# Moving small steps in an attention and adapter kernel: products ahead of scores at lag changes, counts at the end, sums ahead of an output, one store ahead of another

## The chip, the cores and the metric

The kernel runs on one core of a Trainium2 chip. The metric is the device time of one execution in microseconds (us), as a median of several runs. The profile comes from one further execution, recorded by the hardware profiler. The engines are called PE (TensorE matmuls; its weight loads are listed as PEld), DVE (VectorE), ACT (ScalarE), POOL (GpSimd) and SP (SyncE, which here only issues DMAs). An engine works through its own instructions in program order and waits on semaphores of the others.

## The reference

Four batches of 12,288 queries of width 128 attend to 768 keys each. The keys, which are the values too, are 4x4 means of a 384 x 32 map, multiplied by one 128 x 128 matrix. The attention's result goes through a mixture of eight low-rank adapters of rank 16, of which two are chosen for each row.

```python
kv_pool = kv.reshape(B, H // 4, 4, W // 4, 4, C).mean(axis=(2, 4))
k = v = kv_pool.reshape(B, -1, C) @ w_sr
s = (q @ k.transpose(0, 2, 1)) / np.sqrt(C)
a = softmax(s)
x = (a @ v).reshape(B * N, C)               # 49152 x 128
logits = x @ w_gate                         # 8 experts
topk = the two largest of each row;  w = softmax of their logits
out = x + sum over the two: w_k * ((x @ A[e_k]) @ B[e_k])
```

## The kernel before

**Tiling.** The 49,152 queries are 96 chunks of 512 rows (24 chunks to a batch); chunk numbers below are these, and `n` is the last one, 95. A chunk's work has a first and a second half.

First half: `scores(c, r)` multiplies 256 keys by the 512 queries (two matmuls of 512 columns, L329) into one of two score buffers (`stile`, PSUM), and ACT takes the exponential into `tt` (L330). There are three such pairs a chunk. `weigh(c, h)` multiplies the exponentials by the extended values (the values, seven logit columns and a column of ones) into one PSUM buffer, 12 matmuls for each half `h` (L341). `normalise(c)` on DVE takes the reciprocal of the sums of weights (L348), multiplies (L352, which frees the PSUM buffer) and finds the largest logits (L359). `gate` on POOL (L368 to L372) and `gate_tanhs` on ACT make the two gates of each row.

Second half, some chunks later: `turned` transposes the attention rows on PE (L408) into the bank of `t_bank`, from which DVE (L419), in the end ACT (L417), copies them. `gated_hidden` multiplies by A (L443) and applies the gates on DVE (L446). `up` multiplies by B (L489). `give` adds the attention rows (DVE, L503) and issues the store on SP for each pair of chunks (L522). How many chunks later is the `lag`: 9 at the beginning, then 8, 7 and 6 from chunks 57, 67 and 81 on. Where the lag shrinks by one, two products fall into the same iteration: two `gated_hidden` in iterations 65, 74 and 87 and two `up` in iterations 69, 78 and 91. The first of the two uses the bank of `t_bank`, the second the usual bank (`mtile`).

**Order.** All is written out by hand, in the order in which each engine is to work. In iteration `c` of the main loop PE gets: a pair of scores, `weigh(c-1, 0)`, a pair of scores, the first of two `gated_hidden` (where there are two), `up` (one or two), `weigh(c-1, 1)`, the transposes of chunk `c-2`, a pair of scores, the last `gated_hidden`.

**Checks.** The kernel skips the subtraction of the maximum in the softmax. To be safe it counts, over all rows and batches, whether the sums and the values lie in a safe range: `count_ok` and `values_ok` fill `flags`, `count_sum(0)` adds `flags` over the partitions by a matmul with ones (L568) and a copy on ACT (L569), `count_sum(1)` limits eight of the numbers to 1 (L571) and adds them (L572). The last 15 chunks are judged by `tail_ok` on POOL (L575, L576) and counted by `all_ok` on PE (L580, L581); `flag` (DVE, L585 and L587) compares the total with the full count. At the very end all engines read that flag and skip a slow, exact version.

**The tail.** When the main loop is over (iteration 94 is its last), the score buffers are given back and their space becomes the banks `bank(0)`, `bank(1)` and `y5`. The tail finishes chunks 88 to 95 step by step: `weigh(n-1)` and `weigh(n)`, `tops4` (DVE, L834 to L840) in the place of `normalise`; `gate_args` (POOL, L775 to L778), `gate_tanh` (ACT, L781), `gate_w` (POOL, L788, L789); `hidden` (PE, L819), `gated` (DVE, L794), `turn` (PE, L803, copied by ACT at L809 or DVE at L811), `up`; and then either `add_rows` (DVE, L503), or `take` (ACT copies, L494) and `add` (POOL, L498). `put` issues a store of one chunk (256 KB) on SP (L508); the last chunk's goes on ACT's queue. In the last chunk the copy of the transposes is split between ACT and DVE (L811), its two up products are L913 and L918, and the outputs are made by ACT (L915) and DVE (L919).

Of the kernel before, what the change touches and what calls it, by code (L numbers as in the profile page):

```python
# [21 lines left out]
def kernel(  # L22
# [10 lines left out]
    nc = tc.nc  # L33
# [167 lines left out]
    def stile(name):  # L201
        return ps_s.tile([P, 2, NTOK], FP32, tag="sg", name=name)
# [129 lines left out]
    def weigh(c, h, banks=None):  # L332
        b = c // CPB
        if banks is not None:
            xps[c] = banks
        elif h == 0:
            xps[c] = ps_x.tile([P, 2, 512], FP32, tag="x", name="xps")
        for j in range(h * NH, (h + 1) * NH):
            for s in range(NS):
                o = xps[c][:, s // 2, (s % 2) * VW:(s % 2 + 1) * VW]  # L340
                mm(o, tt[c][:, j, s * P:(s + 1) * P], vext[b][:, j, 0:VW],  # L341
                   start=(j == 0 and s % 2 == 0), stop=(j == NJ - 1 and s % 2 == 1),
                   skip_group_check=True)
# [37 lines left out]
    def gate_tanhs(p):  # L381
        gw[p] = gw_all[:, p % 4].rearrange("p e s -> p s e")
        if p < OWN // 2:
            nc.scalar.activation(gw_all[:, p % 4], garg[p].rearrange("p s e -> p e s"), AF.Tanh,
                                 bias=0.0, scale=0.5)
        else:
            th = small.tile([P, 2 * NS, E], FP32, tag="th", name="th")
            nc.scalar.activation(th, garg[p], AF.Tanh, bias=0.0, scale=0.5)
            nc.gpsimd.tensor_scalar(th, th, 1.0, None, op0=ALU.add)
            gw[p] = th  # L390
# [49 lines left out]
    def gated_hidden(c, bank=None):  # L440

        h_ps = mtile([P, NS, P], name="h_ps") if bank is None else as_tokens(bank)
        mm(h_ps, a_bf, xT[c], start=True, stop=True)  # L443
        hgT[c] = run.tile([P, NS, P], BF16, tag="ht", name="ht", bufs=4)
        h = c % 2 * NS // 2
        nc.vector.scalar_tensor_tensor(  # L446
            hgT[c].rearrange("p (k a) t -> p k (a t)", k=2),
            gE[c // 2][:, h:h + NS // 2].rearrange("p a t k -> p k (a t)"), 1.0,
            h_ps.rearrange("p (k a) t -> p k (a t)", k=2), op0=ALU.add, op1=ALU.mult)
# [16 lines left out]
    def apply_gate(c):  # L466
        new_hg(c)
        g = gw[c // 2][:, (c % 2) * NS:(c % 2 + 1) * NS]
        nc.vector.tensor_tensor(
            hg[c].rearrange("p s (r e) -> p s r e", e=E),  # L470
            hps[c].rearrange("p s (r e) -> p s r e", e=E),
            g.unsqueeze(2).broadcast_to([P, NS, RK, E]),
            op=ALU.mult)
# [10 lines left out]
    def up(c, bank=None):  # L484
        fresh = c not in dps
        if fresh:
            dps[c] = mtile([P, NS, P], name="d_ps") if bank is None else as_tokens(bank)
        for s in range(NS):
            mm(dps[c][:, s], columns(hgT[c], c, s), b_bf, start=(s == 0 and fresh),  # L489
               stop=(s == NS - 1), skip_group_check=True)  # L490
# [6 lines left out]
    def add(c, osb, eng):  # L497
        eng.tensor_tensor(osb, osb, xn[c][:, :, 0:C], op=ALU.add)  # L498
# [65 lines left out]

    def count_sum(step):
        if step == 0:
            cnt_ps = stile("cnt_ps")[0:1, 0, 0:2 + 2 * B]
            mm(cnt_ps, ones_c, flags, start=True, stop=True)  # L568
            nc.scalar.activation(cnt, cnt_ps, AF.Copy)  # L569
        else:  # L570
            nc.vector.tensor_scalar(cnt[:, 2:], cnt[:, 2:], 1.0, None, op0=ALU.min)  # L571
            nc.vector.tensor_reduce(tot, cnt, axis=AX.X, op=ALU.add)  # L572

    def tail_ok():
        nc.gpsimd.tensor_scalar(ok[:, tail], rv[:, tail], 1.0 / L_HI, None, op0=ALU.is_ge)  # L575
        nc.gpsimd.tensor_scalar(low, rv[:, tail], 1.0 / L_LO, None, op0=ALU.is_le)  # L576
# [28 lines left out]
    def t_bank():  # L605
        return ps_t.tile([P, NTOK], FP32, tag="tp", name="t_ps")
# [24 lines left out]
    def next_scores():  # L631
        if todo:
            scores(*todo.pop(0))
# [55 lines left out]
    for c in range(2, NCH - 1):  # L689
        b, k = divmod(c, CPB)  # L690
        if c in fetched and lag(2 * fetched[c] + 1) > 8:
            load_gates(fetched[c])
        if c % 2 == 0 and c // 2 + 3 < 2 * NQ:
            turn_q(c // 2 + 3)
        if c % 2 and (c + 11) // 2 < 2 * NQ:
            load_q((c + 11) // 2)
        if c == 2:
            load_q(6)
        next_scores()
        weigh(c - 1, 0)  # L700
        if c == NCH - 2:
            down(c - 4, stile("h_ps")[:, 0])
            apply_gate(c - 4)
        next_scores()
        if c in tanhs:
            gate_tanhs(tanhs[c])
        for x in made.get(c, ())[:-1]:
            gated_hidden(x, t_bank())
        for x in ups.get(c, ()):
            up(x, None if x == ups[c][-1] else t_bank())  # L710
            give(x)
        if c in fetched and lag(2 * fetched[c] + 1) <= 8:
            load_gates(fetched[c])
        weigh(c - 1, 1)
        prep_step(c)
        if c == CUT + 5:
            count_sum(0)
        normalise(c - 1)
        if c % 2 == 0:
            gate(c // 2 - 1, nc.gpsimd)  # L720
            if c // 2 + 4 < 2 * NQ:
                cast_q(c // 2 + 4)
        _, evacuate = turned("x", c - 2)
        if c == NCH - 2:
            _, evacuate_h = turned("h", c - 4, stile("t_ps")[:, 0])
        next_scores()
        prep(c)
        k0 = 19
        if k in (k0, k0 + 2, k0 + 4) and b + 1 < B:
            if b == 0:  # L730
                squares(0, (k - k0) // 2)
            squares(b + 1, (k - k0) // 2)


        early = max(len(made.get(c + 1, ())), len(ups.get(c + 1, ()))) > 1
        if early:
            evacuate()
        for x in made.get(c, ())[-1:]:
            gated_hidden(x)
        if c in sent:  # L740
            send_gates(sent[c])
        if c == NCH - 2:
            down(c - 3, stile("h_ps")[:, 0])
            apply_gate(c - 3)
        if not early:
            evacuate(c == NCH - 2)
        if c == NCH - 2:
            evacuate_h(True)

        if c in (32, 40, 56, 80):  # L750
            ranges((32, 40, 56, 80).index(c))
        a = slice(0, CUT * NS)
        if CUT < c <= CUT + 3:
            count_ok(a, c - CUT - 1, flags[:, 0:1])
        elif c == CUT + 4:
            values_ok()
        elif c == CUT + 7:
            count_sum(1)

# [5 lines left out]
    def bank(i):  # L767
        return ps_e.tile([P, NTOK], FP32, tag=f"e{i}", name=f"e{i}")
# [22 lines left out]
    def gated(c, lo, hi, g, hb):  # L791
        if c not in hg:
            new_hg(c)
        nc.vector.tensor_tensor(  # L794
            hg[c][:, lo:hi].rearrange("p s (r e) -> p s r e", e=E),
            hb.rearrange("p s (r e) -> p s r e", e=E),
            g[:, lo:hi].unsqueeze(2).broadcast_to([P, hi - lo, RK, E]), op=ALU.mult)
# [33 lines left out]
    def tops4(c, top, y):  # L831
# [7 lines left out]
        for s in range(NS):  # L839
            nc.vector.max(top[:, s], xn[c][:, s, C:C + E])  # L840

    gate_tanhs(q_ - 1)
    y4 = ps_x.tile([P, 2, 512], FP32, tag="x", name="y4")
    weigh(n - 1, 0, y4)
# [9 lines left out]
    def fbank(i):  # L854
        return ps_f.tile([P, NTOK], FP32, tag=f"f{i}", name=f"f{i}")
# [5 lines left out]
    up(n - 6, bank(1))  # L861
    o6 = take(n - 6)
    h2 = hidden(n - 3, 0, NS, mtile([P, NTOK], name="h2"))
    up(n - 5, bank(0))
    gate_args(n - 1, 0, NS, nc.gpsimd, top4, arg4, msk4)
    y5 = ps_e.tile([P, 2, 512], FP32, tag="y5", name="y5")
    weigh(n, 0, y5)
    gated(n - 3, 0, NS, gw[q_ - 1][:, 0:NS], h2)
    put(n - 5, add_rows(n - 5))
    add(n - 6, o6, nc.gpsimd)  # L870
# [7 lines left out]
    o1 = take(n - 4)  # L878
    gate_w(0, NS, nc.gpsimd, arg4, msk4)
    tops4(n, top5, y5)  # L880
    tail_ok()
    turn(hg[n - 3], 0, NS, mtile([P, NTOK], name="t2"), hgT, n - 3)
    h4 = hidden(n - 1, 0, NS, bank(1))
    turn(hg[n - 2], 0, NS, t_bank(), hgT, n - 2)
# [10 lines left out]
    h5 = hidden(n, 0, NS, x3[:, 0])  # L895
    turn(hg[n - 1], 0, NS, bank(1), hgT, n - 1)
    gate_w(0, NS, nc.gpsimd, arg5, msk5)
    gated(n, 0, NS, arg5, h5)
    x_first(n - 1, fbank(1), 2, 4)
    d5 = bank(0)  # L900
    x_first(n, d5, 0, 2)
# [2 lines left out]
    turn(hg[n], 2, 4, t_bank(), hgT, n, False)  # L904
    o4 = take(n - 1)
    put(n - 1, o4)
    add(n - 4, o1, nc.gpsimd)
    put(n - 4, o1)
    count = mtile([P, NTOK], name="count")
    all_ok(count)  # L910
    d5 = dps[n]
    for s in range(2):
        mm(d5[:, s], hgT[n][:, s], b_bf, start=False, stop=(s == 1), skip_group_check=True)  # L913
# [2 lines left out]
    d6 = as_tokens(bank(1))  # L916
    for s in range(2, 4):
        mm(d6[:, s - 2], hgT[n][:, s], b_bf, start=(s == 2), stop=(s == 3), skip_group_check=True)  # L918
    nc.vector.tensor_tensor(o5[:, 2:4], d6[:, 0:2], xn[n][:, 2:4, 0:C], op=ALU.add)  # L919
    put(n, o5, queue=nc.scalar)  # L920
    flag(count)
# [127 lines left out]
```

## Time and profile before

| | |
|---|---|
| median of 3 runs | 371.56 us |
| lowest, highest of the runs | 370.53, 2091.47 us |
| the profiled execution | 371.88 us |
| its span, first to last instruction | 370.1 us |
| mean granted TensorE clock | 0.997 |
| PE busy | 355.1 us, 96% |
| ACT busy | 308.7 us, 83% |
| DVE busy | 299.9 us, 81% |
| POOL busy | 223.8 us, 60% |
| DMA moved | 101.01 MB, mean 273 GB/s |

The middle one of the three runs is the time that counts; the highest is an execution by itself and says nothing of the others. A timeline row has the start in us, the duration in us, the engine, the line of the kernel, the operation, what it writes and reads, its shape and how many instructions are merged in it; in brackets stands how long the engine had been idle before it and which engine and line ended that wait. A row of waits has the total, how many and the longest. Matmuls overlap, so the step from one row's start to the next is the time that PE needs for a row; the duration includes the way through the array. The chain of waits follows the work that ended last, back from the end, piece by piece.

### The profile page before, as it was taken

To read this page: it belongs to the slowest core of one execution; us is meant where nothing else is said; L and a number is where in the kernel's file an instruction comes from. 1 tells how busy PE (TensorE), PEld (TensorE's weight loads), DVE (VectorE), ACT (ScalarE), POOL (GpSimd) and SP (SyncE) were. 2 spreads that over 40 slices of the span, in tenths; PEclk is the share of its full clock that TensorE was granted. 3 is DMA by queue.
4 is the path that set the end of the run, shared out by engine and by line. 5 is a ranking of instruction groups with operands and counts; after the bars stand their busy time and mean duration, and the time that the engine had idled before them with its cause. 6 is when DMAs were issued, how large, how long until landed. Compare 5 with 4: busy or idle time off the path is not lost.

```text
span 370.1 us, 10598 instructions
## 1 busy us (share of the span) xinstructions
PE 355.1 (96%) x3944; PEld 263.6 (71%) x3945; DVE 299.9 (81%) x953; ACT 308.7 (83%) x390; POOL 223.8 (60%) x374
## 2 busy tenths in 40 slices
PE   4889999999999999999999999999999999999984
PEld 1446677777777777777777777777777777777773
DVE  3785558888788888888888888888888889989994
ACT  1569998898988898998988988988888889989843
POOL 1013699989589879685477969784544324323253
PEclk9999999999999999999999999999999999999998
DMA  7998999999999999999999999999768789744324
GB/s 251 421 371 200 297 320 320 297 300 290 282 362 303 311 305 332 313 287 262 282 303 336 318 344 309 294 312 250 236 208 250 253 247 223 229 131 131 147 115 174
DMA packets 83818, 101.01 MB, mean 273 GB/s; under 512 B 58804, under 2 KB 59060, under 8 KB 83764
## 3 DMA queue, kind: packets, MB, share of 16 engines
q1 hardware_dynamic: 83332, 99.98, 92.9%
q8 instruction: 31, 0.51, 0.6%
q10 hardware_dynamic: 432, 0.33, 0.3%
q14 instruction: 23, 0.19, 0.2%
HBM read 62.33 MB, written 25.90 MB: 238 GB/s over the span
## 4 chain that ended last, share of the span: by engine, by line
PE 89%; DVE 3%; ACT 3%; DMA 2%; issue 1%; POOL 1%; SPq 0%; ACTq 0%; DVEq 0%
PE xps L341 36%; PE sg L329 33%; PE t_ps L408 6%; PE d_ps L489 5%; PE h_ps L443 5%; DMA kvt<-in_kv_dram 2%; ACT tt L330 2%; PE v_ps L218 1%; DVE kvt L194 1%; PE k_ps L243 1%; PE w_ps L612 1%; PE kp_ps L210 0%; ACT qT L600 0%; DVE xn_all L352 0%; PE y L341 0%
## 5 line engine op out<-in xcount | busy, mean ns | idle before, releaser
L330 ACT ACTIVATE tt<-sg 128x1024 f16<-128x1024 f32 x288 | 276.7, 1022 | 34.6 <-PE sg L329 33.8
L329 PE MATMUL sg<-qT,kfT 128*128 128x512 f16 x576 | 170.3, 379 | 0.6 <-ACT qT L600 0.3
L341 PEld LDWEIGHTS <-tt 128*128 128x128 f16 x2304 | 146.2, 98 | 28.2 <-DVE xn_all L352 17.8
L341 PE MATMUL xps<-vext,tt 128*128 128x136 f16 x2256 | 164.7, 223 | 0.3 <-DVE xn_all L352 0.2
L503 DVE TENSOR_TENSOR osb<-d_ps,xn_all 128x512 f32<-128x512 f32 x85 | 58.7, 691 | 27.7 <-PE d_ps L489 27.1
L368 POOL TENSOR_TENSOR arg<-xn_all,top 128x64 f32<-128x64 f32 x47 | 14.4, 307 | 96.7 <-DVE top L359 81.8
L352 DVE TENSOR_TENSOR xn_all<-xps,rinv_all 128x540 f32<-128x540 f32 x94 | 67.7, 721 | 3.3
L329 PEld LDWEIGHTS <-kfT 128*128 128x128 f16 x576 | 49.1, 98 | 24.6 <-issue 1.8
L194 POOL TENSOR_TENSOR kvt<-kvt 128x1024 f32<-128x1024 f32 x27 | 63.7, 2358 | 2.6 <-PE sg L329 2.6
L108 POOL CAST q<-q 128x1024 f16<-128x1024 f32 x45 | 46.8, 1040 | 24.1 <-DMA q<-in_q_dram 24.1
L446 DVE SCALAR_TENSOR_TENSOR ht<-ge,h_ps 128x512 bf16<-128x512 f16 x87 | 58.5, 672 | 0.4
L489 PEld LDWEIGHTS <-ht 128*128 128x128 bf16 x368 | 27.7, 98 | 21.4 <-DVE ht L446 1.4
L359 DVE MAX8 top<-xn_all 128x8 f32<-128x8 f32 x376 | 35.0, 155 | 6.3
L419 DVE COPY xt<-t_ps 128x512 bf16<-128x512 bf16 x92 | 36.8, 400 | 0.0
L408 PE MATMUL t_ps<-id_bf,xn_all 128*128 128x128 bf16 x376 | 36.4, 219 | 0.0
L489 PE MATMUL d_ps<-b_bf,ht 128*128 128x128 bf16 x340 | 32.9, 220 | 0.0
L443 PE MATMUL h_ps<-xt,a_bf 128*128 128x512 bf16 x86 | 32.6, 379 | 0.1
L348 DVE RECIPROCAL rinv_all<-xps 128x4 f32<-128x4 f32 x94 | 17.1, 182 | 12.9 <-PE xps L341 11.5
L408 PEld LDWEIGHTS <-xn_all 128*128 128x128 bf16 x376 | 25.9, 98 | 0.3
L371 POOL TENSOR_SCALAR msk<-msk 128x64 f32<-128x64 f32 x47 | 20.1, 428 | 4.1
L370 POOL TENSOR_TENSOR arg<-arg,msk 128x64 f32<-128x64 f32 x47 | 15.2, 323 | 3.7
L372 POOL TENSOR_TENSOR arg<-arg,msk 128x64 f32<-128x64 f32 x47 | 15.0, 319 | 3.9
(154 smaller groups left out, 220.5 us busy)
## 6 DMA issues: line engine op xcount, KB each, us to landing
kvt<-in_kv_dram SPq DMA_DIRECT2D x48, 512.0 KB
q<-in_q_dram SPq DMA_DIRECT2D x46, 512.0 KB
out_dram<-osb SPq DMA_DIRECT2D x44, 512.0 KB
ge<-g_h SPq DMA_DIRECT2D x45, 256.0 KB
out_dram<-osb SPq DMA_DIRECT2D x7, 256.0 KB
q<-in_q_dram SPq DMA_DIRECT2D x1, 1024.0 KB
qT<-q SPq DMA_TRANSPOSE x46
g_h<-g_sb SPq DMA_DIRECT2D x45, 16.0 KB
```

What stands on the lines that cost most here:

```text
L108: nc.gpsimd.tensor_copy(q16[i], q32[i].rearrange("p k n -> p (k n)"))
L194: eng.tensor_tensor(v[:, 0], v[:, 0], v[:, d], op=ALU.add)
L329: mm(sg[:, k], kfT[b][:, j * P:(j + 1) * P], qc, start=True, stop=True)
L330: nc.scalar.activation(tt[c][:, 2 * r:2 * r + 2], sg, AF.Exp, bias=0.0, scale=scale)
L341: mm(o, tt[c][:, j, s * P:(s + 1) * P], vext[b][:, j, 0:VW], start=(j == 0 and s % 2 == 0), stop=(j == NJ - 1 and s % 2 == 1), skip_group_ ...
L352: nc.vector.tensor_tensor(xn[c][:, :, 0:C + G].rearrange("p (b s) v -> p b s v", b=2), xv[:, :, :, 0:C + G], ri.rearrange("p (b s) -> p b ...
L408: mm(columns(t_ps, c, s), src[:, s], id_bf, is_transpose=True, start=(s == 0), stop=(s == NS - 1), skip_group_check=True)
L419: nc.vector.tensor_copy(to, t_ps)
L443: mm(h_ps, a_bf, xT[c], start=True, stop=True)
L446: nc.vector.scalar_tensor_tensor(hgT[c].rearrange("p (k a) t -> p k (a t)", k=2), gE[c // 2][:, h:h + NS // 2].rearrange("p a t k -> p k ( ...
L489: mm(dps[c][:, s], columns(hgT[c], c, s), b_bf, start=(s == 0 and fresh), stop=(s == NS - 1), skip_group_check=True)
L503: nc.vector.tensor_tensor(osb[:, lo:hi], d, xn[c][:, lo:hi, 0:C], op=ALU.add)
```

## The change

The first of two products of an iteration now comes ahead of the second pair of scores. With two `up`, the output add and the store of the first (`give`) are written there too. The product with ones of the counts and the copy of its result leave iteration 86 for the first place after the main loop, and use the bank of `t_bank` in place of a score buffer. The limit and the sum of the counts leave iteration 88 for the place behind the last `gated`; the limit is taken by a TENSOR_TENSOR with a broadcast one in place of a TENSOR_SCALAR with a constant. In the tail `up(n - 5)` comes behind the first half of `weigh(n)`. The add and the store of chunk n-4 come ahead of those of chunk n-1; `tail_ok` moves behind that add on POOL, and `all_ok` behind the last up products on PE.

```diff
     def count_sum(step):
         if step == 0:
-            cnt_ps = stile("cnt_ps")[0:1, 0, 0:2 + 2 * B]
+            cnt_ps = t_bank()[0:1, 0:2 + 2 * B]
             mm(cnt_ps, ones_c, flags, start=True, stop=True)
             nc.scalar.activation(cnt, cnt_ps, AF.Copy)
         else:
-            nc.vector.tensor_scalar(cnt[:, 2:], cnt[:, 2:], 1.0, None, op0=ALU.min)
+            nc.vector.tensor_tensor(cnt[:, 2:], cnt[:, 2:],
+                                    ones_c[0:1, 0:1].broadcast_to([1, 2 * B]), op=ALU.min)
             nc.vector.tensor_reduce(tot, cnt, axis=AX.X, op=ALU.add)
...
+
+        for x in made.get(c, ())[:-1]:
+            gated_hidden(x, t_bank())
+        for x in ups.get(c, ())[:-1]:
+            up(x, t_bank())
+            give(x)
         next_scores()
         if c in tanhs:
             gate_tanhs(tanhs[c])
-        for x in made.get(c, ())[:-1]:
-            gated_hidden(x, t_bank())
-        for x in ups.get(c, ()):
-            up(x, None if x == ups[c][-1] else t_bank())
+        for x in ups.get(c, ())[-1:]:
+            up(x)
             give(x)
...
-        if c == CUT + 5:
-            count_sum(0)
...
-        elif c == CUT + 7:
-            count_sum(1)
...
+    count_sum(0)
     gate_tanhs(q_ - 1)
     y4 = ps_x.tile([P, 2, 512], FP32, tag="x", name="y4")
     weigh(n - 1, 0, y4)
...
     h2 = hidden(n - 3, 0, NS, mtile([P, NTOK], name="h2"))
-    up(n - 5, bank(0))
     gate_args(n - 1, 0, NS, nc.gpsimd, top4, arg4, msk4)
     y5 = ps_e.tile([P, 2, 512], FP32, tag="y5", name="y5")
     weigh(n, 0, y5)
+    up(n - 5, bank(0))
...
     tops4(n, top5, y5)
-    tail_ok()
...
     gate_w(0, NS, nc.gpsimd, arg5, msk5)
+    add(n - 4, o1, nc.gpsimd)
+    put(n - 4, o1)
+    tail_ok()
     gated(n, 0, NS, arg5, h5)
+    count_sum(1)
...
     o4 = take(n - 1)
     put(n - 1, o4)
-    add(n - 4, o1, nc.gpsimd)
-    put(n - 4, o1)
-    count = mtile([P, NTOK], name="count")
-    all_ok(count)
...
         mm(d6[:, s - 2], hgT[n][:, s], b_bf, start=(s == 2), stop=(s == 3), skip_group_check=True)
+    count = mtile([P, NTOK], name="count")
+    all_ok(count)
     nc.vector.tensor_tensor(o5[:, 2:4], d6[:, 0:2], xn[n][:, 2:4, 0:C], op=ALU.add)
```

## The prediction

> **What bounds the kernel now.** I read the chain of waits first, by engine, on the page.
>
> ```profile
> PE 89%; DVE 3%; ACT 3%; DMA 2%; issue 1%; POOL 1%; SPq 0%; ACTq 0%; DVEq 0%
> ```
>
> Nine tenths of the chain is TensorE, so in the loop only an edit that takes time from PE, or a stall out of it, counts. The second view was the chain piece by piece, where each half of a chunk's weighted sums (twelve L341 matmuls) is one piece.
>
> ```profile
> 250.62 0.71 PE xps L341 x12
> 252.64 0.87 PE xps L341 x12
> ...
> 267.38 0.75 PE xps L341 x12
> ...
> 343.37 0.87 PE xps L341 x12
> ```
>
> A piece is 0.71 us wherever PE runs through. Late in the kernel six pieces are longer: five read 0.87, from the one at 252.64 to the one at 343.37, and are 0.16 over; one reads 0.75, 0.04 over. They stand right behind chunks 65, 69, 74, 78, 87 and 91, which are the six in which the lag of the second half of the work (gate product, up product, store) shrinks and two products fall into one chunk instead of one. The timelines of PE and VectorE at chunk 87 show what happens there.
>
> ```profile
> 326.41 0.60 PE L329 MATMUL sg<-qT,kfT 128*128 128x512 f16 x2
> 326.85 0.38 PE L443 MATMUL t_ps<-xt,a_bf 128*128 128x512 bf16 x1
> ...
> 329.45 0.88 PE L341 MATMUL xps<-vext,tt 128*128 128x136 f16 x12
> ```
>
> ```profile
> 325.95 0.68 DVE L446 SCALAR_TENSOR_TENSOR ht<-ge,h_ps 128x512 bf16<-128x512 f16 x1
> 327.26 0.69 DVE L446 SCALAR_TENSOR_TENSOR ht<-ge,t_ps 128x512 bf16<-128x512 f16 x1 [0.63 <-PE t_ps L443]
> 327.87 0.68 DVE L503 TENSOR_TENSOR osb<-d_ps,xn_all 128x512 f32<-128x512 f32 x1
> 328.47 0.17 DVE L348 RECIPROCAL rinv_all<-xps 128x4 f32<-128x4 f32 x1
> 328.67 0.72 DVE L352 TENSOR_TENSOR xn_all<-xps,rinv_all 128x540 f32<-128x540 f32 x1
> ```
>
> DVE stands 0.63 us for the extra product, then works without a gap through gate, output add and normalisation. The normalisation ends at 328.67 + 0.72 = 329.39, and only then may PE write the single bank of sums: at 329.45. That wait is the 0.16 of the piece behind chunk 87.
>
> **The change part by part.**
>
> *Products ahead of the scores.* In the six chunks the extra product moves in front of one pair of score matmuls, so it starts 0.43 earlier (the step of a pair of scores, 326.85 - 326.41) and the scores start later by the product's own step, an estimated 0.22: the scores' 0.43 for two matmuls of 512 columns, halved for the product's one. No instruction is added; order on DVE, ACT and SP stays. At chunk 87 the gate multiplication can start behind the one at 325.95 instead of at 327.26. The output add then waits for its own product and the reciprocal for its sums, which arrive about 0.27 before the 328.47 of now. A normalisation ending 0.27 sooner removes a wait of 0.16 entirely; 0.11 is left over. The other chunks are in the grouped waits (total us, times, longest): three gate products and three up products, with VectorE idle ahead of each.
>
> ```profile
> DVE osb L503 <- PE t_ps L489: 1.5, 3, 0.9
> DVE ht L446 <- PE t_ps L443: 1.2, 3, 0.6
> ```
>
> With 0.63 and 0.9 for the longest, 0.3 a chunk is left for the others, about twice the 0.16 that has to go. Gain: 5 x 0.16 + 0.04 = 0.84 us. The delayed scores cost nothing as long as ACT has idle time ahead of them; the chain gives ACT 3%, so in most chunks it isn't ACT that is late.
>
> What speaks for a cost is the one bank ("t_bank") that the product shares with the transposes before it. The tightest chunk is 74:
>
> ```profile
> 281.02 0.41 DVE L419 COPY xt<-t_ps 128x512 bf16<-128x512 bf16 x1
> ```
>
> ```profile
> 281.50 0.38 PE L329 MATMUL sg<-qT,kfT 128*128 128x512 f16 x1
> ```
>
> The copy frees the bank at 281.43; the product would now start at 281.50, where the scores do. A hand-over from DVE to PE took 0.06 above (329.39 to 329.45), so it fits by 0.01. I take nothing; the bound is a few hundredths a chunk.
>
> *Counts.* The counting product leaves chunk 86, and its two VectorE operations chunk 88.
>
> ```profile
> 323.46 0.87 PE L341 MATMUL xps<-vext,tt 128*128 128x136 f16 x12
> 324.26 0.20 PE L568 MATMUL cnt_ps<-flags,ones_c 128*1 128x10 f32 x2
> 324.39 0.40 PE L408 MATMUL t_ps<-id_bf,xn_all 128*128 128x128 bf16 x4
> ```
>
> From the sums to the transposes it is 324.39 - 323.46 = 0.93 instead of the 0.71 of a piece: 0.22 us of PE, gained whole, as PE is the bound there. The VectorE pair stood before an output add in a chunk whose sums are no longer than 0.71, so taking it away gives nothing. In the tail the product comes back, behind the bank's evacuation by ACT and ahead of the sums of chunk 94:
>
> ```profile
> 352.88 0.38 PE L457 MATMUL h_ps<-a_bf,xt 128*128 128x128 bf16 x4
> 353.51 0.89 PE L341 MATMUL y<-vext,tt 128*128 128x136 f16 x12 [0.25 <-DVE xn_all L352]
> ```
>
> ```profile
> 352.44 0.60 ACT L417 ACTIVATE xt<-t_ps 128x512 bf16<-128x512 bf16 x1 [0.83 <-PE t_ps L408]
> ```
>
> The bank is free at 353.04 and PE at about 353.10; 0.22 of counting ends by 353.32, before the 353.51 at which the sums may start. That wait covers it; without cover it would cost 0.22. ACT's small copy (ten numbers) follows its evacuations, with nothing urgent behind it on ACT: bounds 0 and 0.1. Loop in all: 0.84 + 0.22 = 1.06 us.
>
> *Sums ahead of an output.* In the tail the engine that is busy without a gap is DVE, until it waits once for PE:
>
> ```profile
> 359.17 0.69 DVE L794 TENSOR_TENSOR hgs<-t_ps,th 128x512 bf16<-128x512 f32 x1 [0.41 <-PE t_ps L819]
> ```
>
> ```profile
> 356.74 0.39 PE L819 MATMUL h<-a_bf,xt 128*128 128x128 bf16 x4
> 357.59 0.38 PE L489 MATMUL e<-b_bf,ht 128*128 128x128 bf16 x4 [0.46 <-ACT ht L417]
> ```
>
> PE stands 0.46 in the up product of chunk 90, waiting for ACT, with the first half of the last sums behind it. Put first, the sums run in that hole (356.96 to 357.67) and the product follows at 357.67, 0.08 later than now, which is the most that its output add can lose. The product of chunk 93 for which DVE waits (t_ps, L819), which stands behind all these on PE, comes 0.4 sooner, so the 0.41 goes. Behind it DVE has no gap until 363.78 (its next idle time is the 0.56 quoted below), so the shift is passed on. Gain 0.41; bounds 0 and 0.46. What is late next is DVE itself.
>
> *Store of chunk 91 ahead of chunk 94, checks behind.* The last stores and what moves them:
>
> ```profile
> 363.01 1.27 POOL L498 TENSOR_TENSOR osb<-osb,xn_all 128x512 f32<-128x512 f32 x1
> ```
>
> ```profile
> 365.11 0.81 SPq L508 DMA_DIRECT2D out_dram<-osb  x2
> ...
> 365.59 0.36 ACTq L508 DMA_DIRECT2D out_dram<-osb  x1
> ```
>
> ```profile
> 365.50:366.00 0.50, 0.00 (x0) 0.00 (x0) 0.32 (x3) 0.00 (x0) 0.00 (x0) 1.00 0.08 33
> 366.00:366.50 0.50, 0.00 (x0) 0.00 (x0) 0.00 (x0) 0.00 (x0) 0.00 (x0) 1.00 1.03 381
> ...
> 368.00:368.50 0.50, 0.00 (x0) 0.00 (x0) 0.00 (x0) 0.00 (x0) 0.00 (x0) 0.50 0.34 94
> ```
>
> (The last two columns of the stretches are the busy share of the DMA engines and GB/s.) Chunk 91's output is ready when POOL's add ends, 364.28, but SP issues it behind chunk 94, at 365.11 + 0.4. So three stores of 256 KB go out as one full burst, 366.0 to 368.2, and the program ends when that burst has landed. Issued on its own, chunk 91 leaves between 364.3 and 365.9, when the DMA engines are idle, and the burst is two stores: less 262,144 B / 380 GB/s = 0.69, I take 0.70 (bounds 0 and 0.83, the latter if the burst of two starts with the full rate at 365.95). The checks lie beside: tail_ok follows the add on POOL, and the counting products run behind the last up product while DVE does the last add. The flag then comes as it does now, right behind that add, before either of the last two stores has moved its data. The two VectorE count operations fall into the idle time that this row shows ahead of the last copy:
>
> ```profile
> 364.34 0.29 DVE L811 COPY xr<-t_ps 128x256 bf16<-128x256 bf16 x1 [0.56 <-PE t_ps L803]
> ```
>
> It is 0.56 us wide, from 363.78 on. The old pair took
>
> ```profile
> 333.92 0.30 DVE L571 TENSOR_SCALAR cnt<-cnt 1x8 f32<-1x8 f32 x1
> 334.26 0.15 DVE L572 TENSOR_REDUCE tot<-cnt 1x1 f32<-1x10 f32 x1
> ```
>
> 0.49 from the start of one to the end of the other. The new form (a TENSOR_TENSOR with two SBUF inputs) isn't in the trace at this size; I take the same 0.3, bounds 0.06 and what the first rival gives. So the pair is covered.
>
> One rule bears against this place. The Trainium skill, page "SBUF — State Buffer", section "Who interferes with whom", says that a VectorE instruction with two SBUF inputs contends with a GpSimd instruction that reads SBUF: an exclusive lock held for the whole instruction. No row of this trace shows the lock by itself; and L571, whose 0.30 us is twice the reduction's 0.15, would fit it. By the rule the time would be that of the first rival, without it that of the forecast.
>
> Sum: 1.06 + 0.41 + 0.70 = 2.17 us. The profiled execution took 371.88 (span 370.1), which would become 369.7. The median of the runs shown, 371.56, lies 0.3 below that; from it the forecast is **369.4 us**, 0.6% faster.
>
> **The rivals.** *The count operation is held by POOL's add.* The add runs from 363.01 to 364.28 and the operation wants to start at 363.78. If it can't before 364.28, it and the reduction (together some 0.3) end near 364.6, the copy of 364.34 and with it the last output go 0.25 later. Part of that hides behind chunk 94's store: 369.6. For it: both stand in the same place, the add directly behind the gate that releases DVE. This is what the SBUF page's lock would do.
>
> *The loop gives nothing.* The 0.22 by which the scores are late, six times, could pass to ACT's exponentials and come back as later sums. Then 1.11 to 1.33 is left: 370.3. Against it: the chain, by engine, has ACT at 3%.
>
> *The end gives nothing*, because the store on ACT's queue alone sets it: 1.47 is left, 370.1. Against it: that store is one third of the burst.
>
> *Slower: the bank isn't free at the copy.* If the moved product's wait is counted to the VectorE instruction behind the copy (the gate multiplication, which ends at 325.95 + 0.68 = 326.63 in chunk 87 against a new start near 326.19), PE stands 0.5 us in five of the six chunks with the scores behind it: 2.5 lost and 0.84 not gained. Against 1.33 from the rest that is 1.2 slower, 372.8. It decides from a stand of 0.36 a chunk upward (2.17/6).
>
> **How the numbers follow.** Forecast 0.55; operation held 0.18; loop nothing 0.14; end nothing 0.08; slower 0.04; 0.01 for anything else. The runs of before lie between 370.53 and 371.88, a spread I give to the new ones as well: 370.53 less the largest sum (1.06 + 0.46 + 0.83) is 368.2, and 371.88 with half a microsecond gained is 371.4. Range 368.1 to 371.5; the slower rival lies outside. Over 2% (7.4 us), about what a measurement of this kernel can tell from no change, nothing here reaches: within 2% 0.97, faster 0.01, slower 0.02.
>
> **What would show it.** Right: the six pieces read 0.71; the extra products' VectorE operations lose their idle time; no L568 near 324 and about 1.06 less at the last exponential; no 0.41 ahead of the L794; the last stretch of full DMA rate lasts 1.4 us instead of 2.1. Wrong: a PE wait on VectorE ahead of a t_ps product (the bank), more than 0.56 between L794 and the last L811 copy (the count operation), a chunk's sums waiting for ACT.

## The result and the profile after

The changed kernel takes 369.46 us (median of 7 runs, 369.23 to 370.12) against 371.56: a ratio of 0.995, 95% interval 0.9938 to 0.9963. Its profiled execution took 369.38 us with a span of 367.5, which is 2.6 less than before. The page of the changed kernel, its chain by engine:

```profile
span 367.5 us, 10597 instructions
...
PE 91%; DVE 3%; ACT 2%; DMA 1%; POOL 1%; issue 1%; ACTq 0%
```

The chain piece by piece, at the six places behind the iterations with two products:

```profile
252.69 0.71 PE xps L341 x12
...
267.33 0.71 PE xps L341 x12
...
284.45 0.71 PE xps L341 x12
...
298.19 0.71 PE xps L341 x12
...
328.80 0.71 PE xps L341 x12
...
342.54 0.71 PE xps L341 x12
```

All six read 0.71; none is longer any more. Chunk 87 on DVE, in the same order as before:

```profile
325.53 0.68 DVE L446 SCALAR_TENSOR_TENSOR ht<-ge,h_ps 128x512 bf16<-128x512 f16 x1
326.17 0.69 DVE L446 SCALAR_TENSOR_TENSOR ht<-ge,t_ps 128x512 bf16<-128x512 f16 x1
326.83 0.69 DVE L503 TENSOR_TENSOR osb<-d_ps,xn_all 128x512 f32<-128x512 f32 x1
327.54 0.18 DVE L348 RECIPROCAL rinv_all<-xps 128x4 f32<-128x4 f32 x1
327.75 0.72 DVE L352 TENSOR_TENSOR xn_all<-xps,rinv_all 128x540 f32<-128x540 f32 x1
```

The second gate multiplication follows the first 0.64 us later instead of 1.31, with no idle time in brackets, and from the first of them to the normalisation it is 2.22 instead of 2.72.

In the tail, DVE around the gate of chunk 93 and at the end:

```profile
357.71 0.68 DVE L795 TENSOR_TENSOR hgs<-t_ps,th 128x512 bf16<-128x512 f32 x1
358.31 0.17 DVE L835 RECIPROCAL rinv_all<-y 128x4 f32<-128x4 f32 x1
...
361.51 0.69 DVE L795 TENSOR_TENSOR hgs<-x,r 128x512 bf16<-128x512 f32 x1
362.12 0.61 DVE L571 TENSOR_TENSOR cnt<-cnt,ones_c 1x8 f32<-1x8 f32 x1
362.76 0.15 DVE L573 TENSOR_REDUCE tot<-cnt 1x1 f32<-1x10 f32 x1
362.84 0.29 DVE L812 COPY xr<-t_ps 128x256 bf16<-128x256 bf16 x1
363.51 0.42 DVE L922 TENSOR_TENSOR osb<-e,xn_all 128x256 f32<-128x256 f32 x1 [0.38 <-PE e L919]
```

The 0.41 us of idle time ahead of L795 (L794 before) is gone. The counts' limit (L571) now takes 0.61 us, not 0.3.

**Where the time went.** The start of an execution and its last stores vary from profile to profile, so I compare stretches between instructions in between. The marks are the reciprocal of chunk 60 (ahead of every edit), that of chunk 92 (behind the loop's edits), that of chunk 95 (L834 or L835) and the last VectorE add (L919 or L922). Of before and after, the first two marks:

```profile
236.96 0.18 DVE L348 RECIPROCAL rinv_all<-xps 128x4 f32<-128x4 f32 x1
...
349.01 0.18 DVE L348 RECIPROCAL rinv_all<-xps 128x4 f32<-128x4 f32 x1
```

```profile
237.01 0.18 DVE L348 RECIPROCAL rinv_all<-xps 128x4 f32<-128x4 f32 x1
...
348.03 0.18 DVE L348 RECIPROCAL rinv_all<-xps 128x4 f32<-128x4 f32 x1
```

The last two marks of before (those of after stand among the rows above):

```profile
359.88 0.18 DVE L834 RECIPROCAL rinv_all<-y 128x4 f32<-128x4 f32 x1
...
365.08 0.43 DVE L919 TENSOR_TENSOR osb<-e,xn_all 128x256 f32<-128x256 f32 x1 [0.45 <-PE e L918]
```

| stretch, us | before | after | gain |
|---|---|---|---|
| chunk 60 to chunk 92 | 112.05 | 111.02 | 1.03 |
| chunk 92 to chunk 95 | 10.87 | 10.28 | 0.59 |
| chunk 95 to the last add | 5.20 | 5.20 | 0.00 |
| last add to the end of the span | 5.02 | 3.99 | 1.03 |

The first three rows repeat within 0.02 us wherever the code in them is the same; the last one doesn't, as the experiments show.

### The profile page after: what moved, and what is told of

Read it like the earlier page. It is cut to its first block, busy times and chain, and to the rows that moved or that the text cites. A ratio compares the mean times of both kernels' runs of the same rounds, so it can differ in the third digit from the quotient of the medians.

```text
span 367.5 us, 10597 instructions
## 1 busy us (share of the span) xinstructions
PE 354.9 (97%) x3945; PEld 264.4 (72%) x3945; DVE 300.2 (82%) x953; ACT 308.5 (84%) x390; POOL 223.8 (61%) x374
## 4 chain that ended last, share of the span: by engine, by line
PE 91%; DVE 3%; ACT 2%; DMA 1%; POOL 1%; issue 1%; ACTq 0%
PE xps L341 36%; PE sg L329 33%; PE t_ps L408 5%; PE d_ps L489 5%; PE h_ps L443 5%; PE w_ps L613 2%; ACT tt L330 2%; PE v_ps L218 1%; DMA w_gate_sb<-in_moe_w_gate_dram 1%; PE k_ps L243 1%; DVE osb L503 1%; DVE ht L446 1%; PE kp_ps L210 0%; ACT qT L601 0%; DVE xn_all L836 0%
```

## The experiments

The four parts went into the kernel before one at a time, and then some together or out of the changed kernel again. All readings of the stretches stand in one table behind them.

**The products alone** (the hunk of the main loop).

> The kernel before, with only the extra products moved ahead of the scores. My theory (VectorE idles for the extra product and the next sums wait for its normalisation): the six long pieces of the chain (five of 0.87, one of 0.75 us) all read 0.71, and the span falls by 0.84 us, to about 369.3. Rival (the delayed scores pass the time on to ACT): the pieces shrink but the last exponential of the loop comes no earlier, span 370.1.

Runs 370.96 us against 371.57, ratio 0.9986 (0.9977 to 0.9995). From chunk 60 to 92 it takes 111.26: a gain of 0.79, and nothing more behind. The six pieces all read 0.71. The theory holds; if the delayed scores cost anything, it is within the 0.05 that is missing from 0.84.

**The store with the checks alone.**

```diff
     tops4(n, top5, y5)
-    tail_ok()
...
     gate_w(0, NS, nc.gpsimd, arg5, msk5)
+    add(n - 4, o1, nc.gpsimd)
+    put(n - 4, o1)
+    tail_ok()
...
     put(n - 1, o4)
-    add(n - 4, o1, nc.gpsimd)
-    put(n - 4, o1)
-    count = mtile([P, NTOK], name="count")
-    all_ok(count)
...
+    count = mtile([P, NTOK], name="count")
+    all_ok(count)
     nc.vector.tensor_tensor(o5[:, 2:4], d6[:, 0:2], xn[n][:, 2:4, 0:C], op=ALU.add)
```

> The kernel before, with only the add and store of chunk 91 ahead of those of chunk 94, and with them the tail checks behind that add and the counting products behind the last up products. My theory (the end is the last burst, three stores, and one of them leaves earlier): everything up to the last VectorE add as before, the last burst at full rate some 0.7 to 0.85 us shorter, span 369.1 to 369.4. In the changed kernel the end came 1.02 us closer to the last VectorE add, more than a store's 0.70; if this one also gives 1.0, the term itself was too small and no other part is behind it. Rival (the store on ACT's queue alone sets the end): span 370.1.

In the profile the end came 0.71 us closer to the last add (4.31), as expected. The runs were no faster: 371.58 against 371.57, ratio 1.0003 (0.9993 to 1.0014), scattered from 370.55 to 372.43. This miss led to three more runs below.

**The sums alone** (`up(n - 5, bank(0))` behind `weigh(n, 0, y5)`).

> The kernel before, with only the first half of the last weighted sums ahead of the up product of chunk 90. My theory: the 0.41 us of VectorE's idle time ahead of the gate of chunk 93 goes, and the last VectorE add comes 0.4 to 0.6 us earlier (0.58 in the changed kernel), span 369.5 to 369.7. Rival (what is gained is taken by the next wait, for the gates from POOL, where tail_ok still stands in front): the gate multiplication of chunk 95 starts no more than 0.2 earlier, span 369.9 or more.

Runs 371.47, ratio 1.0 (0.9992 to 1.0009): no gain. DVE and POOL of this kernel:

```profile
358.58 0.69 DVE L794 TENSOR_TENSOR hgs<-t_ps,th 128x512 bf16<-128x512 f32 x1
...
362.91 0.69 DVE L794 TENSOR_TENSOR hgs<-x,r 128x512 bf16<-128x512 f32 x1 [0.40 <-POOL r L789]
```

```profile
360.48 0.36 POOL L575 TENSOR_SCALAR ok<-rinv_all 128x60 f32<-128x60 f32 x1
360.80 0.36 POOL L576 TENSOR_SCALAR low<-rinv_all 128x60 f32<-128x60 f32 x1
361.12 0.25 POOL L775 TENSOR_TENSOR r<-xn_all,top 128x32 f32<-128x32 f32 x1
```

The idle time ahead of the gate of chunk 93 has gone, 0.45 us by chunk 95. Then DVE waits 0.40 us for POOL, which is late with the gates of chunk 95 because `tail_ok` (L575, L576) stands in front of them. The gain comes back as a new wait: the rival was right for this part alone.

**The counts alone** (the hunks of `count_sum` and its four calls).

> The kernel before, with only the counts moved out of the loop and limited by a TENSOR_TENSOR. My theory: 0.22 us of PE goes from chunk 86, nothing comes back ahead of the sums of chunk 94; the limit takes about 0.6 us as in the changed kernel, because it starts while POOL's add runs and ends with it; the last copy is up to 0.1 later behind it, which the last up product hides, since it waits for ACT; span 369.9. Rival (the held operation is on the path): the 0.22 are lost again to it, span 370.1 or more.

Runs 371.47, ratio 0.9996 (0.9987 to 1.0004). The loop gives 0.22, as expected. The tail gives 0.23 more by chunk 95, which I had not seen; 0.09 of it is lost again by the last add (5.29 instead of 5.20). The 0.36 that is left there is within what these runs can't tell from nothing. In the kernel before, PE waited for DVE ahead of the up product of chunk 88 (quoted from its timeline); with the counts moved it doesn't:

```profile
355.10 0.38 PE L489 MATMUL e<-b_bf,ht 128*128 128x128 bf16 x4 [0.23 <-DVE hgs L469]
```

```profile
353.82 0.38 PE L443 MATMUL h_ps<-xt,a_bf 128*128 128x512 bf16 x1
354.04 0.38 PE L489 MATMUL e<-b_bf,ht 128*128 128x128 bf16 x4
```

The score buffers alternate, and the counting product no longer takes one; that the tail's bank 0 therefore lies over the other buffer, which is free sooner, I infer from the code and from this wait.

**The sums and the store together**, products and counts as before.

> The kernel before with two parts together, the sums ahead of the output and the store with the checks behind it; products and counts as before. Theory (the sums alone gained 0.04 us at the last VectorE add because tail_ok stood in front of the gates of chunk 95 on POOL; the store's part moves it away): the gate multiplication of chunk 95 no longer waits for POOL and the last VectorE add comes 0.4 to 0.5 us earlier than before, seen from the same early instruction; with the shorter burst the runs are about 1.1 us faster. Rival (another wait is behind POOL's): less than 0.2 us at the last add.

Runs 370.79 against 371.73, ratio 0.9975 (0.9965 to 0.9985): 0.94 us faster, about as expected. The gate of chunk 95 has no wait left:

```profile
362.09 0.69 DVE L503 TENSOR_TENSOR osb<-f,xn_all 128x512 f32<-128x512 f32 x1
362.77 0.69 DVE L794 TENSOR_TENSOR hgs<-x,r 128x512 bf16<-128x512 f32 x1
```

All of 0.44 us reaches the last add. So the sums' gain needs `tail_ok` out of POOL's way, which only the store's part brings.

**The store behind again**, in the changed kernel: `put(n - 4, o1)` back behind `put(n - 1, o4)`, the add and the checks where they are.

> The changed kernel with one thing undone: the store of chunk 91 is issued behind that of chunk 94 again (its add stays where it is). Theory (three stores in the last burst instead of two, 0.7 us more): the last VectorE add at the same time as in the changed kernel, the last burst 0.6 to 0.8 us longer, runs 0.5 to 0.9 us slower than the changed kernel's, so about 0.997 of the kernel before. Rival, from the runs of the store alone, which were no faster (what the shorter burst gives is lost again between its end and the program's end): runs as those of the changed kernel, 0.995.

Runs 369.68, ratio 0.9952 (0.9938 to 0.9965), where 0.997 was expected. The changed kernel has 0.995 and, measured once more (below), 369.62 and 0.9948. So the runs show some 0.1 us for this store, as the rival says, though intervals of half a microsecond either way don't exclude the expected loss. The kernel with POOL's limit (below), on the same chip, was 0.55 faster, but it differs in the limit too. In the profile the last add comes when it did, and the end is at 4.71 from it, instead of 3.99 and 4.42 in the changed kernel's two profiles.

**The store alone, without the checks.**

```diff
     gate_w(0, NS, nc.gpsimd, arg5, msk5)
+    add(n - 4, o1, nc.gpsimd)
+    put(n - 4, o1)
...
     put(n - 1, o4)
-    add(n - 4, o1, nc.gpsimd)
-    put(n - 4, o1)
```

> The kernel before with only the add and the store of chunk 91 ahead of those of chunk 94; checks and counting products stay where they were. The part with the checks gave 0.7 us in its profile and nothing in its runs, which is open. Theory (the shorter last burst counts in every execution, and those runs scattered): last VectorE add as before, the program's end 0.6 to 0.8 us closer to it, runs 0.4 to 0.7 us faster, 0.998 to 0.999. Rival (alone the store gives nothing in the runs, only together with an earlier flag does the end move): runs 1.000.

Runs 370.91 against 371.55, ratio 0.9986 (0.9977 to 0.9996): 0.6 us faster. The end is at 4.54. So alone the store does show in the runs. Why the kernel with the checks moved as well showed nothing stays open.

**A longer add on POOL**, in the changed kernel.

```diff
-    spare = []
+    spare, whole = [], {}
...
+            whole[0] = o
...
     o1 = take(n - 4)
+    o01 = whole[0].rearrange("p k s c -> p (k s) c")
...
-    add(n - 4, o1, nc.gpsimd)
+    nc.gpsimd.tensor_tensor(o01, o01, xpair[(n - 4) // 2][:, :, 0:C], op=ALU.add)
```

(`whole[0]` is the pair of output buffers of which `o1` is one half.)

> The changed kernel with POOL's add of chunk 91 made twice as wide: it also adds chunk 90's rows to chunk 90's finished output buffer, which is not stored again, so the operation takes about 2.36 us instead of 1.27. Theory (the limit of the counts is held until the running POOL operation ends): the limit takes about 1.7 us instead of 0.61 and ends with the add, and the last copy behind it is about 1.0 us late. Rival (a TENSOR_TENSOR of this form with a broadcast operand takes 0.6 us by itself): 0.6 us, the last copy where it was.

One execution, 369.57 us. The add on POOL, and then DVE:

```profile
360.90 2.35 POOL L901 TENSOR_TENSOR osb<-osb,xn_all 128x1024 f32<-128x1024 f32 x1
```

```profile
361.59 1.69 DVE L572 TENSOR_TENSOR cnt<-cnt,ones_c 1x8 f32<-1x8 f32 x1
363.31 0.15 DVE L574 TENSOR_REDUCE tot<-cnt 1x1 f32<-1x10 f32 x1
```

The add ends at 363.25 and the limit at 363.28. In the changed kernel the add on POOL ran from 361.43 to 362.70 and the limit ended at 362.73:

```profile
361.43 1.27 POOL L498 TENSOR_TENSOR osb<-osb,xn_all 128x512 f32<-128x512 f32 x1
```

An operation on eight numbers ends when the other engine's operation ends, 0.01 to 0.03 us behind it in all five profiles that have both: it is held, and 0.6 us is no fixed time of this form. As expected, the last copy comes 1.08 us late here (2.41 behind the start of the last gate multiplication instead of 1.33), and the last add comes 1.07 late with it. From there to the end it is 3.75 us, less than in any other profile, and the one execution is about at the changed kernel's medians (369.46 and 369.62).

**The limit on POOL**, in the changed kernel, and once more beside the changed kernel itself.

```diff
         else:
-            nc.vector.tensor_tensor(cnt[:, 2:], cnt[:, 2:],
-                                    ones_c[0:1, 0:1].broadcast_to([1, 2 * B]), op=ALU.min)
             nc.vector.tensor_reduce(tot, cnt, axis=AX.X, op=ALU.add)
...
     count_sum(0)
     gate_tanhs(q_ - 1)
+    nc.gpsimd.tensor_scalar(cnt[:, 2:], cnt[:, 2:], 1.0, None, op0=ALU.min)
```

> The changed kernel with the limit of the counts done by POOL in its idle time at the start of the tail (0.3 us, TENSOR_SCALAR), so that VectorE has only the reduction behind the last gate multiplication. Theory: the last copy comes 0.08 us earlier, and the last VectorE add not at all, since its up product waits for ACT's copy; time as the changed kernel. Rival (the held limit was on the path): the last VectorE add 0.1 us or more earlier.

> The changed kernel once more, to stand beside the next one on the same chip and to give a second profile of its end. Theory: 0.9945, within its interval of 0.9938 to 0.9963; from the last VectorE add to the end 4.0 to 4.3 us (3.99 in its first profile, 4.31 with the store alone, 4.6 to 5.0 in the kernels that store chunk 91 last). If it is over 4.5, the store's gain in the first profile was scatter.

> The changed kernel with the limit of the counts done by POOL, on the same chip as the changed kernel. Theory (the held limit delays only a copy that another wait hides): the same time as the changed kernel within 0.2 us. Rival: 0.3 us faster, as its first runs were (369.13 against 369.46 on another chip).

With the limit on POOL: 369.13 us, 0.994 (0.9926 to 0.9954), and 369.34, 0.9943 (0.993 to 0.9957). The changed kernel beside the second of these: 369.62, 0.9948 (0.9936 to 0.9961), with 4.42 us from the last add to the end, above the expected 4.0 to 4.3. The limit on POOL may make the kernel 0.3 faster; the intervals overlap, and neither the theory nor the rival is excluded. DVE with the limit on POOL:

```profile
361.33 0.69 DVE L793 TENSOR_TENSOR hgs<-x,r 128x512 bf16<-128x512 f32 x1
361.94 0.14 DVE L571 TENSOR_REDUCE tot<-cnt 1x1 f32<-1x10 f32 x1
362.58 0.29 DVE L810 COPY xr<-t_ps 128x256 bf16<-128x256 bf16 x1 [0.50 <-PE t_ps L802]
363.32 0.42 DVE L921 TENSOR_TENSOR osb<-e,xn_all 128x256 f32<-128x256 f32 x1 [0.45 <-PE e L918]
```

From the last gate multiplication to the copy it is 1.25 us instead of 1.33, and to the last add 1.99 instead of 2.00. The held limit costs the copy 0.08 us and the last add nothing.

The readings (stretches in us; the marks are those of the section above):

| kernel | 60 to 92 | 92 to 95 | 95 to last add | last add to end | chunk 91's store |
|---|---|---|---|---|---|
| before | 112.05 | 10.87 | 5.20 | 5.02 | last |
| products alone | 111.26 | 10.86 | 5.22 | 4.57 | last |
| counts alone | 111.83 | 10.64 | 5.29 | 4.73 | last |
| sums alone | 112.05 | 10.42 | 5.61 | 4.90 | last |
| sums and store | 112.05 | 10.43 | 5.20 | 4.23 | earlier |
| changed | 111.02 | 10.28 | 5.20 | 3.99 | earlier |

The distance from the last add to the end in the others: store behind again 4.71; store with checks 4.31, store alone 4.54, limit on POOL 3.98 and 4.44, the changed kernel again 4.42. With the store last it lies between 4.57 and 5.02 (five profiles, mean 4.79), with the store earlier between 3.98 and 4.54 (seven, mean 4.27; the kernel with the longer add left out). The two groups lie side by side without overlapping, and their means are 0.52 apart.

The scatter sits for the most part in one wait, that of SP at the end of the program for the last stores (total us, times, longest). In the kernel before, in the changed kernel and in the changed kernel again it is:

```profile
SPq L1044 <- DMA out_dram<-osb: 1.1, 1, 1.1
```

```profile
SPq L1047 <- DMA out_dram<-osb: 0.2, 1, 0.2
```

```profile
SPq L1047 <- DMA out_dram<-osb: 0.6, 1, 0.6
```

The two profiles of the changed kernel differ by 0.4 in this wait and by 0.43 in the distance. With chunk 91's store last the wait is 0.7 to 1.1 in the five profiles. With the store earlier it is 0.6 three times, 0.5 (in two waits), 0.4 and 0.2, and in the first profile with the limit on POOL there is none. What makes the same stores land later in one execution than in another isn't known.

## Why the prediction was right, point by point

**The bound and the products: right, with the mechanism and nearly the size.** 0.84 was forecast and 0.79 measured alone. The six pieces fell to 0.71. DVE's idle time ahead of the extra products' operations, 1.5 and 1.2 us before, went but for one wait, behind which the piece reads 0.71 all the same:

```profile
DVE osb L503 <- PE t_ps L489: 0.5, 1, 0.5
```

The bank shared with the transposes was in time, in chunk 74 too.

**The counts in the loop: right**, 0.22 forecast and measured. Costing their return in the tail at nothing held as well. What I missed is a third effect, the 0.23 us in the tail that came with the changed turn of the score buffers. It overlaps with the sums' gain: 0.45 alone and 0.23 alone give 0.59 together.

**The sums: the term came out, but a step of its reasoning failed.** "Behind it DVE has no gap until 363.78, so the shift is passed on" is not true of the edit by itself: passed on alone, it met POOL, and 0.41 of 0.45 was lost again. I had looked for gaps on DVE and not at when its other inputs would be ready. In the kernel before, DVE's output add and POOL's gates of chunk 95 ended together (363.09 and 363.05):

```profile
362.40 0.69 DVE L503 TENSOR_TENSOR osb<-f,xn_all 128x512 f32<-128x512 f32 x1
```

```profile
362.80 0.25 POOL L789 TENSOR_TENSOR r<-r,r 128x32 f32<-128x32 f32 x1
```

POOL had 0.7 us of `tail_ok` ahead of its gates. I had counted the move of `tail_ok` as a check that "lies beside"; it is what makes the sums' gain reach the end. The whole term was then 0.59 with the buffers' effect, against 0.41 and a bound of 0.46.

**The store: right in kind, too large in size.** The term was 0.70, worked out from a full rate for one store. The groups of profiles give 0.52. The runs give 0.3 to 0.5: the changed kernel is 2.10 and 1.93 us faster, and 1.62 of that it has gained by the last add. The store alone gave 0.6 in the runs. Two kernels speak against it and aren't explained: with the checks moved too, and with the store put back in the changed kernel, the runs show 0.0 and 0.1. The first profile's 1.03 was in good part scatter: the same kernel showed 4.42 instead of 3.99 in its second one. The burst itself did become shorter. The DMA engines of the changed kernel:

```profile
363.50:364.00 0.50, 0.27 (x4) 0.09 (x2) 0.49 (x2) 0.28 (x2) 0.00 (x0) 1.00 0.82 324
364.00:364.50 0.50, 0.00 (x0) 0.00 (x0) 0.25 (x2) 0.00 (x0) 0.00 (x0) 1.00 0.78 291
364.50:365.00 0.50, 0.00 (x0) 0.00 (x0) 0.00 (x0) 0.00 (x0) 0.00 (x0) 1.00 1.04 393
365.00:365.50 0.50, 0.00 (x0) 0.00 (x0) 0.00 (x0) 0.00 (x0) 0.00 (x0) 1.00 0.99 377
365.50:366.00 0.50, 0.00 (x0) 0.00 (x0) 0.00 (x0) 0.00 (x0) 0.00 (x0) 1.00 0.57 217
```

The full rate lasts some 1.3 us from 364.5 on, as forecast, but chunk 91's store goes directly ahead of it and not in idle time. In the kernel before, too, the engines were still busy to 0.97 from 364.0 to 364.5, where the prediction calls them idle. That the mean gain stays under 0.70 shows in SP's wait: in three of the seven profiles with the store earlier it is still 0.6. One execution suggests how little an earlier landing could add: in the kernel with the longer add SP has no wait for a store left at the end, and 3.75 us from the last add remain.

**The first rival: it happened, and cost nothing up to the last add.** The operation was held until POOL's add ended, and 0.61 us instead of 0.3 is what that rival says. The sign given for it came too: from the end of the gate multiplication to the last copy it is 0.64 us, more than 0.56. Its price (0.25 at the copy and in part at the end) was too high. It had the two operations take 0.3 us behind the end of the add; in fact the copy began 0.14 behind it, and was only 0.08 late. The last up product behind it waits for ACT's copy in any case, as the up product's row of the changed kernel shows:

```profile
363.07 0.29 PE L914 MATMUL e<-b_bf,xr 128*128 128x128 bf16 x2 [0.41 <-ACT xr L810]
```

Whether the runs lose anything by the hold is open: with the limit on POOL they were 0.2 to 0.4 us faster by the ratios, within the intervals. Nor was the 0.30 us of the old form surely its time alone: in the kernel before it ran from 333.92 to 334.22, beside a POOL operation from 333.88 to 334.20.

By the rule of the Trainium skill, page "SBUF — State Buffer", section "Who interferes with whom", a VectorE instruction with two SBUF inputs and a GpSimd instruction that reads SBUF exclude each other. The runs agree, with 0.61 and 1.69 us beside adds of 1.27 and 2.35. The reduction, with one input, took 0.14 us beside the running add.

**The sum.** 1.06 + 0.41 + 0.70 = 2.17 was forecast. Measured by stretches it is 1.03 + 0.59 + 0.52 = 2.14, and by the medians 2.10 and 1.93. The total is better than its parts, and that is luck: the sums' term was too low and the store's too high by about the same.

## What to carry to other kernels

Read a gain at one engine through to the end by asking, for each later instruction, which of its inputs is ready just in time; two chains that end together share the next gain only if both are shortened. When edits are tested alone, expect some to show nothing until another has moved what stands behind them. And where start-up and last transfers scatter by half a microsecond, compare stretches between two fixed instructions: they showed the 0.36 us of the counts alone, which eleven runs could not.

## What the runs showed of the hardware

A VectorE TENSOR_TENSOR on 1 x 8 numbers in SBUF took 0.61 and 1.69 us, ending 0.03 us after the POOL operation that was running when it began. Time between fixed instructions inside the kernel repeats to 0.02 us across profiles, while the distance from the last add to the end varied by 0.4 for the same code (3.99 and 4.42), as did SP's wait for the last stores (0.2 and 0.6).
